# The head of a fused spectral and feed-forward kernel: squares, transforms and products in another order, and the last down weights in six pieces

## The chip, the cores and the metric

The kernel runs on one core of a Trainium2 chip. The metric is the device time of one execution in microseconds (us). The engines are TensorE (PE in the profile, with PEld for its weight loads), VectorE (DVE), ScalarE (ACT), GpSimd (POOL) and SyncE (SP), which here issues nearly all transfers.

## The reference

```python
def _A_ref(x, w_r, w_i):
    X = rfft2(x.astype(float32), axes=(-2, -1))
    W = w_r + 1j * w_i
    return irfft2(X * W, s=(S, D), axes=(-2, -1)).astype(bfloat16)

def _B_ref(x, w_gate, w_up, w_down):
    return (_gelu(x @ w_gate) * (x @ w_up)) @ w_down

h = x + _A_ref(_layernorm(x), A_w_r, A_w_i)
return h + _B_ref(_layernorm(h), B_w_gate, B_w_up, B_w_down)
```

S is 2048 rows, D is 576 columns and the hidden width is 4608. Everything is bf16. The input `B_x` is not used. The first line is a filter in the frequency domain, done with matrix products; the second is a gated feed-forward layer.

## The kernel before, in words

The 2048 rows lie in `h_sb` as 16 tiles of 128 rows; tile h holds the rows h, h + 16 and so on. The spectral part transforms, multiplies by the weights and transforms back. Its last step is a transform over the columns, `inv_cols(x, g)`, for two halves x and eight groups g: ten matrix products into a PSUM buffer and one copy out, on ACT except for (1, 1), which is on DVE. `add_rows(g)` then combines both halves of group g into two PSUM buffers, one for tile 2g and one for 2g + 1, and these are added to `h_sb`.

All of these PSUM buffers, those of the turns and those of the feed-forward products have one tag, `two`, with four buffers. They are handed out in turn in the order of the program, so a matrix product that opens a buffer waits until the reader of the buffer four openings earlier is done.

The feed-forward part works on four blocks of 512 rows (`tcnk`). For each of them `gate` computes 36 column blocks f of the hidden width: 18 matrix products for gate and up, a Gelu on ACT into `g_sb` and a multiplication on DVE (L895) into `P_sb`. Then the down products of four tiles follow, with the weights `wd[f // 12]`, which lie in three parts of 12 blocks. Gate and up weights come in groups of three column blocks (`load_gu`, two transfers each) into three buffers; group n is loaded when the last block of group n - 3 is done.

The head is the seam of the two parts. So that PE need not wait until four tiles are ready, the first eight column blocks of the first 512 rows are done in two halves: first for tiles 0 and 1 (the loop over `NH`), and later, as the first eight blocks of the main loop, for tiles 2 and 3. Tiles 0 and 1 get their mean and variance from a sum that comes with the addition (`add_sum`) and a sum of squares (`sum_squares`, on ACT), put together by `head_rstd` (three small instructions on DVE and a power on POOL). They are normalised (`norm_row`), transposed by PE (`turn_mm`) and copied into the layout that `gate` reads by DVE (`turn_out`). Tiles 2 and 3 are normalised by `norm2` and transposed by a transfer (`flip`, issued by SP).

The order of each engine is that of the program text: the schedule is manual. Work of the main loop that is not a product is put in by the table `todo`, whose key is the number of the block behind which it is issued: the folding and adding of later tiles, their statistics, their normalised rows and their flips. The table `after` does the same for the eight first half blocks. SP has one queue and works in order of the program: an issue that waits holds up the issues behind it.

Of the kernel before, what the change touches and what calls it, by code (L numbers as in the profile page):

```python
# [9 lines left out]
ACT = mybir.ActivationFunctionType  # L10
ALU = mybir.AluOpType
FP32 = mybir.dt.float32
BF16 = mybir.dt.bfloat16
# [7 lines left out]
P = 128  # L21
S = 2048
H = 16
D = 576
# [17 lines left out]
def kernel_body(  # L42
# [11 lines left out]
    nc = tc.nc  # L54
    V = nc.vector
    A = nc.scalar
# [4 lines left out]
    keep = ctx.enter_context(tc.tile_pool(name="keep", bufs=1))  # L61
    wgpool = ctx.enter_context(tc.tile_pool(name="wgu", bufs=3))
    roll = ctx.enter_context(tc.tile_pool(name="roll", bufs=2))
    psum = ctx.enter_context(tc.tile_pool(name="psum", bufs=1, space=bass.MemoryType.PSUM))

    def two(name):
        return psum.tile([P, 2, 512], FP32, name=name, tag="two", bufs=4)

    h_sb = keep.tile([P, H, D], BF16, name="h_sb")
# [6 lines left out]
    def const(name, val):  # L76
        t = keep.tile([P, 1], FP32, name=name)
        V.memset(t[:], val)
        return t

    zerob = const("zerob", 0.0)
# [30 lines left out]
    sums = keep.tile([P, H, 2], FP32, name="sums")  # L112
# [43 lines left out]
    wd_view = B_w_down.rearrange("(ft p) d -> p ft d", p=P)  # L156
    NWA = 12
# [479 lines left out]
    def inv_cols(x, g):  # L637

        ps = two("cs_ps")
        for w in range(NW):  # L640
            for e in range(2):
                rows = slice(64 * e, 64 * e + JW)
                T.matmul(  # L643
                    ps[:, e, 0:JP],
                    lhsT=EO[x][rows, w, 2 * g : 2 * g + 2].rearrange("p h e k l -> p (h e k l)"),
                    rhs=DQ[rows, w] if w or e else DT[rows, 0, :, 0, :],
                    start=(w == 0),
                    stop=(w == NW - 1),
                )
        pv = ps[:, :, 0:JP].rearrange("p t (q a) -> p t q a", q=2)  # L650
        if g >= 2:
            if x == 0 or g == 2:
                cw[x, g] = eop.tile([P, 2, JP], FP32, name=f"cw{x}{g}")[:]
            else:
                cw[x, g] = cwb[:, g - 3]
            A.activation(
                cw[x, g].rearrange("p t (a q) -> p t q a", q=2), pv, ACT.Copy, scale=Y_SCALE
            )
            return
        ts = eop.tile([P, 2, JP], BF16, name=f"cs{x}{g}")  # L660
        dst = ts[:].rearrange("p t (a q) -> p t q a", q=2)
        if x == 1 and g == 1:
            V.tensor_scalar(dst, pv, Y_SCALE, None, op0=ALU.mult)
        else:
            A.activation(dst, pv, ACT.Copy, scale=Y_SCALE)
        cs[x, g] = ts
# [58 lines left out]
    wd = [wd_a] + [fp.tile([P, NWA, D], BF16, name=f"wd_{i}") for i in range(2)]  # L725

    def load_wd(i):
        nc.sync.dma_start(wd[i][:], wd_view[:, i * NWA : (i + 1) * NWA, :])
# [5 lines left out]

    load_wd(1)


    ln2 = {}
    both = {}
# [13 lines left out]
    def add_rows(g):  # L753


        ys = [two("y_ps") for _ in range(2)]
        sl = (slice(0, DH), slice(DH, 0, -1))
        for x in range(2):
            for b in range(2):
                for t in range(2 if g < 2 else 1):  # L760
                    for i in range(2):
                        rows = slice(64 * i, 64 * i + 64)
                        T.matmul(  # L763
                            ys[i][:, b, 0:DH],
                            lhsT=G16[rows, b * t, x, :],
                            rhs=cs[x, g][rows, t, sl[b]] if g < 2 else both[x, g][rows, b, :],
                            start=(x == 0 and t == 0),
                            stop=(x == 1 and (g >= 2 or t == 1)),
                        )
        return ys  # L770
# [33 lines left out]
    def add_sum(h, ys, squares=True):  # L804


        hv = h_sb[:, h, :].rearrange("p (b n) -> p b n", b=2)
        V.scalar_tensor_tensor(  # L808
            hv, ys[h % 2][:, :, 0:DH], 1.0, hv, op0=ALU.mult, op1=ALU.add, accum_out=sums[:, h, 0:1]
        )  # L810
        if squares:
            sum_squares(h)

    def sum_squares(h):
        junk = roll.tile([P, D], BF16, name="junk", tag="junk", bufs=2)
        A.activation(junk[:], h_sb[:, h, :], ACT.Square, scale=float(D) ** 0.5, accum_out=sums[:, h, 1:2])  # L816

    def head_rstd(h):


        V.scalar_tensor_tensor(
            mv2[:, h, 1:2], sums[:, h, 0:1], sums[:, h, 0:1], sums[:, h, 1:2], op0=ALU.mult, op1=ALU.subtract
        )
        V.tensor_scalar(rstd2[:, h : h + 1], mv2[:, h, 1:2], -1.0 / (D * D), 1e-5, op0=ALU.mult, op1=ALU.add)
        V.tensor_scalar(mv2[:, h, 0:1], sums[:, h, 0:1], 1.0 / D, None, op0=ALU.mult)
        G.tensor_tensor(rstd2[:, h : h + 1], rstd2[:, h : h + 1], mhalf[:, h : h + 1], ALU.pow)  # L826

    def turn_mm(h):
        pt = psum.tile([P, 2048], BF16, name="pt", tag="two", bufs=4)
        for r in range(NR):  # L830
            for p0 in (0, 64):
                T.transpose(pt[p0 : p0 + 64, r * P : (r + 1) * P], ln2[h][:, r * 64 : (r + 1) * 64], ident[:])  # L832
        return pt
# [5 lines left out]
    def norm_row(h):  # L839
        hrow = ln2[h] = roll.tile([P, D], BF16, name="hflat", tag="hrow", bufs=4)  # L840
        normalise(V, hrow[:], mv2, rstd2, h)

    inv_cols(1, 0)
    inv_cols(1, 1)
    A.activation(keep.tile([P, 1], FP32, name="first_gelu")[:], zerob[:], ACT.Gelu_apprx_tanh)
    y0 = add_rows(0)
    add_sum(0, y0)
    add_sum(1, y0)
    head_rstd(0)
    head_rstd(1)  # L850
    for x, g in ((0, 6), (0, 7), (1, 2), (1, 3)):
        inv_cols(x, g)
    norm_row(0)
    norm_row(1)
    pt0 = turn_mm(0)
    inv_cols(1, 4)
    pt1 = turn_mm(1)
    turn_out(0, pt0)
    turn_out(1, pt1)
# [5 lines left out]
    todo = {}  # L865
    for h in range(4, H):
# [6 lines left out]
        todo.setdefault(b, []).append((norm2, h))  # L873
        todo.setdefault(b + 1, []).append((flip, h))

    blk = 0
    groups = pre
    NG = NFT // FQ

    def gate(tcnk, f, w, i, lo, hi):  # L880
        n = hi - lo
        gu = two("gu")
        for r in range(NR):
            for c in range(2):
                rows = slice(64 * c, 64 * c + 64)
                T.matmul(  # L886
                    gu[:, c, 0:n],
                    lhsT=w[rows, r, i * P : (i + 1) * P],
                    rhs=hl[tcnk % 2][rows, r, lo:hi],
                    start=(r == 0),  # L890
                    stop=(r == NR - 1),
                )
        g_sb = roll.tile([P, D], FP32, name="g_sb", tag="g_sb", bufs=3)[:, 0:n]
        A.activation(g_sb, gu[:, 0, 0:n], ACT.Gelu_apprx_tanh)  # L894
        V.tensor_tensor(p_sb(f)[:, lo:hi], g_sb, gu[:, 1, 0:n], ALU.mult)  # L895

    NH = 8
    after = {
        0: [(sum_squares, 3), (norm2, 2), (flip, 2), (head_rstd, 3)],
        1: [(norm2, 3), (flip, 3), (load_wd, 2)],  # L900
    }
    for f in range(NH):
        gate(0, f, groups[f // FQ], f % FQ, 0, 2 * P)
        for fn, h in after.get(f, ()):
            fn(h)
        if 2 <= f <= 4:
            inv_cols(1, f + 3)
    for tcnk in range(4):
        for gi in range(NG):
            for i in range(FQ):  # L910
                f = gi * FQ + i
# [51 lines left out]
@with_exitstack  # L963
def kernel(
    ctx: ExitStack,
    tc: tile.TileContext,
    A_x: bass.AP,
    A_w_r: bass.AP,
    A_w_i: bass.AP,
    B_x: bass.AP,  # L970
    B_w_gate: bass.AP,
    B_w_up: bass.AP,
    B_w_down: bass.AP,
    out: bass.AP,
):
    kernel_body(tc, A_x, A_w_r, A_w_i, B_x, B_w_gate, B_w_up, B_w_down, out)
# [30 lines left out]
```

## Time and profile before

| what | value |
|---|---|
| median of three runs | 500.94 us (500.82 to 501.02) |
| the profiled execution | 501.55 us |
| its span | 499.8 us |
| PE busy | 489.0 us, 98% of the span |
| DVE, ACT, POOL busy | 222.7, 162.9, 29.2 us |
| granted clock of TensorE | 1.0 in all of the span |
| PE busy, 62.0 to 79.15 us | 15.76 of 17.15 us |
| PE busy, 79.15 to 90.4 us | 10.50 of 11.25 us |
| PE busy, 90.4 to 145 us | 54.60 of 54.60 us |
| mean share of the transfer engines, 104 to 133.25 us | 1.08, 193 GB/s |

Times in the profile count from the start of the span. The span is what the engines were seen to do; the execution's own time has some microseconds around it. The views used are the page, the waits (who stood still until whom, in all, how often and the longest), the chain of waits (the work that ended last, followed back), the timeline (start, duration, engine, line, operation, count and in brackets the idle time before it with what ended it) and windows (the busy time of each engine, the granted clock, the share of the transfer engines in use and GB/s, in a stretch of time). The ends of matrix products are modelled, and neighbours overlap by about 0.2 us.

### The profile page before, as it was taken

How to read it: one execution, taken by the hardware profiler on the slowest of the kernel's cores; microseconds unless marked ns; L12 is line 12 of the kernel's file. 1: busy time of each engine (PE TensorE's matmuls, PEld its weight loads, DVE VectorE, ACT ScalarE, POOL GpSimd, SP SyncE). 2: the span in 40 equal slices, each digit the busy share in tenths (PEclk: the TensorE clock that was granted, in tenths of full speed). 3: DMA queues.
4: the chain of work that ended last, by engine and by line, in shares of the span. 5: the costliest groups of instructions: out<-in, count | busy, mean ns of one | idle time of the engine just before them, and what ended most of it. 6: DMA issues, size and time to landing. Idle time of an engine off the chain costs nothing.

```text
span 499.8 us, 12608 instructions
## 1 busy us (share of the span) xinstructions
PE 489.0 (98%) x5644; PEld 321.5 (64%) x5644; DVE 222.7 (45%) x440; ACT 162.9 (33%) x289; POOL 29.2 (6%) x78
## 2 busy tenths in 40 slices
PE   7999989999999999999999999999999999999997
PEld 3567779444469964444499944444799644445995
DVE  8989776788641235433311154333211333333111
ACT  8989973222320112323300133232110223233000
POOL 8500010111110000000000000000000000000000
PEclk9999999999999999999999999999999999999999
DMA  8729749999971019998740069987700287770000
GB/s 285 217 60 201 213 129 230 182 168 199 172 151 24 2 49 172 200 181 153 160 87 3 3 147 193 196 159 155 146 3 1 71 157 155 156 153 2 14 13 25
DMA packets 89469, 62.33 MB, mean 125 GB/s; under 512 B 23110, under 2 KB 88006, under 8 KB 89414
## 3 DMA queue, kind: packets, MB, share of 16 engines
q1 hardware_dynamic: 89126, 60.34, 59.6%
q0 software_dynamic: 288, 1.18, 0.7%
q8 instruction: 44, 0.72, 0.6%
q14 instruction: 11, 0.09, 0.1%
HBM read 52.65 MB, written 2.36 MB: 110 GB/s over the span
## 4 chain that ended last, share of the span: by engine, by line
PE 89%; DMA 2%; DVE 1%; ACT 0%; POOL 0%; issue 0%; SPq 0%; ACTq 0%
PE gu L886 54%; PE acc L928 26%; PE cs_ps L643 2%; PE acc L947 2%; PE eo_ps L592 2%; DMA wgu<-in_B_w_up_dram 2%; PE pq_ps L478 1%; PE y_ps L763 1%; PE gh_ps L496 0%; PE gh_ps L495 0%; DVE hrow L788 0%; PE pt L832 0%; PE eo_ps L616 0%; POOL rstd L826 0%; ACT junk L816 0%; DVE h_sb L808 0%
## 5 line engine op out<-in xcount | busy, mean ns | idle before, releaser
L886 PE MATMUL gu<-Bt,wgu 64*128 64x512 bf16 (+1 forms) x2736 | 284.1, 365 | 1.4 <-DMA wgu<-in_B_w_up_dram 0.7
L886 PEld LDWEIGHTS <-wgu 64*128 64x128 bf16 x2736 | 136.4, 94 | 145.2 <-DMA wgu<-in_B_w_up_dram 1.2
L895 DVE TENSOR_TENSOR P_sb<-g_sb,gu 128x512 bf16<-128x512 f32 (+1 forms) x152 | 99.6, 657 | 145.9 <-ACT g_sb L894 145.9
L894 ACT ACTIVATE g_sb<-gu 128x512 f32<-128x512 f32 (+1 forms) x152 | 87.3, 575 | 195.3 <-PE gu L886 195.1
L928 PEld LDWEIGHTS <-P_sb 64*128 64x128 bf16 x2160 | 132.7, 94 | 0.6
L928 PE MATMUL acc<-wd,P_sb 64*128 64x288 bf16 x1440 | 93.8, 283 | 0.0
L937 DVE TENSOR_TENSOR part<-part,acc 128x576 f32<-128x576 f32 x15 | 11.3, 754 | 111.3 <-ACT part L936 111.3
L928 PE MATMUL acc<-wd_a,P_sb 64*128 64x288 bf16 x720 | 49.7, 283 | 0.0
L936 ACT COPY part<-acc 128x576 f32<-128x576 f32 x15 | 9.6, 639 | 122.4 <-PE acc L928 122.4
L285 PE MATMUL f2t<-h_sb,ident 128*128 128x512 bf16 x27 | 9.1, 501 | 3.6 <-DMA h_sb<-in_A_x_dram 3.6
L478 PE MATMUL pq_ps<-DT,Bt 128*128 128x290 bf16 x64 | 12.2, 286 | 0.2 <-DVE Bt L327 0.2
L788 DVE TENSOR_SCALAR hrow<-h_sb,mv,rstd 128x1152 bf16<-128x1152 bf16 x14 | 12.1, 867 | 0.6 <-POOL rstd L826 0.6
L939 DVE TENSOR_TENSOR h_sb<-h_sb,part 128x576 bf16<-128x576 bf16 x15 | 11.4, 758 | 0.5
L643 PE MATMUL cs_ps<-DQ,EO 58*128 58x290 bf16 x144 | 11.3, 283 | 0.0
L133 POOL TENSOR_TENSOR rstd<-rstd,mhalf 128x1 f32<-128x1 f32 (+1 forms) x16 | 11.2, 701 | 1.3
L478 PEld LDWEIGHTS <-Bt 128*128 128x128 bf16 x96 | 9.3, 97 | 2.6
L132 POOL TENSOR_SCALAR rstd<-mv 128x1 f32<-128x1 f32 (+1 forms) x16 | 3.9, 246 | 102.6 <-DVE mv L118 102.4
L297 PE MATMUL f2t<-F,xn 128*128 128x256 bf16 x64 | 9.2, 274 | 0.6 <-DVE xn L136 0.6
L489 ACT CAST pq<-pq_ps 128x580 bf16<-128x580 f32 x15 | 9.6, 668 | 0.0
L123 ACT ACTIVATE junk<-h_sb 128x576 bf16<-128x576 bf16 x14 | 9.4, 676 | 0.4 <-DMA h_sb<-in_A_x_dram 0.4
L643 PEld LDWEIGHTS <-EO 58*128 58x128 bf16 x160 | 8.0, 94 | 2.0 <-issue 0.4
L117 DVE BATCH_NORM_STATS2 st<-h_sb 128x6 f32<-128x288 bf16 x21 | 9.3, 441 | 0.0
(133 smaller groups left out, 266.0 us busy)
## 6 DMA issues: line engine op xcount, KB each, us to landing
wgu<-in_B_w_gate_dram SPq DMA_DIRECT2D x48, 432.0 KB
wgu<-in_B_w_up_dram SPq DMA_DIRECT2D x48, 432.0 KB
wd<-in_B_w_down_dram SPq DMA_DIRECT2D x2, 1728.0 KB
wd_a<-in_B_w_down_dram SPq DMA_DIRECT2D x1, 1728.0 KB
out_dram<-h_sb SPq DMA_DIRECT2D x3, 576.0 KB
h_sb<-in_A_x_dram SPq DMA_DIRECT2D x4, 288.0 KB
h_sb<-in_A_x_dram SPq DMA_DIRECT2D x2, 576.0 KB
WR<-in_A_w_r_dram SPq DMA_DIRECT2D x1, 650.2 KB
```

The source lines that it names most:

```text
L133: G.tensor_tensor(dst[:, sl], dst[:, sl], mhalf[:, sl], ALU.pow)
L478: T.matmul(ps[:, par, 0:JP], lhsT=Bt[:, t, col], rhs=DT[:, t // 2, par] if t < 4 else DF[:, par], start=(t == par), stop=(t == 4),)
L592: T.matmul(pv[:, n], lhsT=z[:, a, w].rearrange("p b j -> p (b j)"), rhs=TI[:, ts[k], 1 - a : 3 - a, :], start=(a == 0), stop=(a == 1),)
L643: T.matmul(ps[:, e, 0:JP], lhsT=EO[x][rows, w, 2 * g : 2 * g + 2].rearrange("p h e k l -> p (h e k l)"), rhs=DQ[rows, w] if w or e else DT ...
L788: V.tensor_scalar(hrow[:], h_sb[:, h, :].rearrange("p (r k) -> p r k", k=64).unsqueeze(2).to_broadcast([P, NR, 2, 64]), mv2[:, h, 0:1], rs ...
L886: T.matmul(gu[:, c, 0:n], lhsT=w[rows, r, i * P : (i + 1) * P], rhs=hl[tcnk % 2][rows, r, lo:hi], start=(r == 0), stop=(r == NR - 1),)
L894: A.activation(g_sb, gu[:, 0, 0:n], ACT.Gelu_apprx_tanh)
L895: V.tensor_tensor(p_sb(f)[:, lo:hi], g_sb, gu[:, 1, 0:n], ALU.mult)
L928: T.matmul(accs[i][:, c, 0:DH], lhsT=p_sb(f)[rows, st * P : (st + 1) * P], rhs=wd[f // NWA][rows, f % NWA, c * DH : (c + 1) * DH], start=( ...
L937: V.tensor_tensor(part, part, accs[1][:, :, 0:DH], ALU.add)
L939: V.tensor_tensor(hv, hv, part, ALU.add)
L947: T.matmul(acc[:, 0, 0:DH], lhsT=p_sb(f)[:, st * P : (st + 1) * P], rhs=wd[f // NWA][:, f % NWA, cc], start=(f == 0), stop=(f == NFT - 1),)
```

## The change

Seven things are different, all between the last column transforms and the middle of the first 36 blocks.

- The squares of tile 1 are computed by DVE, with one instruction that multiplies the tile by itself and sums up, instead of by ACT.
- Six column transforms, (0, 6), (0, 7) and (1, 2) to (1, 5), stand between the addition of tiles 0 and 1 and their turns. Before, four stood there, (1, 4) stood between the two turns and (1, 5) behind the third gate block.
- The two turns follow each other.
- The first Gelu, which brings ACT's table load, comes behind the copies of these six transforms.
- In the half blocks, `head_rstd(3)` comes behind block 1 instead of block 0, and tile 3's row and its flip behind block 2 instead of block 1.
- (1, 6) and (1, 7) come behind half blocks 2 and 3, where before (1, 5) to (1, 7) came behind 2 to 4.
- The last third of the down weights, which was one transfer behind tile 3's flip, is six transfers of two blocks each, behind blocks 10, 13, 16, 19, 22 and 25 of the main loop.

```diff
+    def load_wd2(s):
+        nc.sync.dma_start(wd[2][:, s], wd_view[:, 2 * NWA : 3 * NWA][:, s])
...
     inv_cols(1, 0)
     inv_cols(1, 1)
-    A.activation(keep.tile([P, 1], FP32, name="first_gelu")[:], zerob[:], ACT.Gelu_apprx_tanh)
     y0 = add_rows(0)
     add_sum(0, y0)
-    add_sum(1, y0)
+    add_sum(1, y0, squares=False)
+    for x, g in ((0, 6), (0, 7), (1, 2), (1, 3), (1, 4), (1, 5)):
+        inv_cols(x, g)
+    A.activation(keep.tile([P, 1], FP32, name="first_gelu")[:], zerob[:], ACT.Gelu_apprx_tanh)
+    junk = roll.tile([P, D], BF16, name="junk", tag="junk", bufs=2)
+    V.scalar_tensor_tensor(
+        junk[:], h_sb[:, 1, :], float(D), h_sb[:, 1, :], op0=ALU.mult, op1=ALU.mult, accum_out=sums[:, 1, 1:2]
+    )
     head_rstd(0)
     head_rstd(1)
-    for x, g in ((0, 6), (0, 7), (1, 2), (1, 3)):
-        inv_cols(x, g)
     norm_row(0)
     norm_row(1)
     pt0 = turn_mm(0)
-    inv_cols(1, 4)
     pt1 = turn_mm(1)
     turn_out(0, pt0)
     turn_out(1, pt1)
...
+    for i in range(0, NWA, 2):
+        todo.setdefault(10 + 3 * i // 2, []).append((load_wd2, slice(i, i + 2)))
...
     after = {
-        0: [(sum_squares, 3), (norm2, 2), (flip, 2), (head_rstd, 3)],
-        1: [(norm2, 3), (flip, 3), (load_wd, 2)],
+        0: [(sum_squares, 3), (norm2, 2), (flip, 2)],
+        1: [(head_rstd, 3)],
+        2: [(norm2, 3), (flip, 3)],
     }
     for f in range(NH):
         gate(0, f, groups[f // FQ], f % FQ, 0, 2 * P)
         for fn, h in after.get(f, ()):
             fn(h)
-        if 2 <= f <= 4:
-            inv_cols(1, f + 3)
+        if 2 <= f <= 3:
+            inv_cols(1, f + 4)
```

## The prediction

> **What bounds the kernel now.** I read the page first: PE is busy for 98% of the span and the granted clock is 1.0 everywhere, so only time in which PE stands still, or order that makes it stand still, can be won. Then the waits of 58 to 95 us, the stretch that the edit touches.
>
> ```profile
> PE gu L886 <- DMA wgu<-in_B_w_up_dram: 0.7, 1, 0.7
> PE pt L832 <- DVE hflat L136: 0.7, 1, 0.7
> PE gu L886 <- DVE P_sb L895: 0.7, 1, 0.7
> ```
>
> Three waits of PE. The timeline of PE places them:
>
> ```profile
> 62.00 0.28 PE L643 MATMUL cs_ps<-DT,EO 58*128 58x290 bf16 x1
> ...
> 65.39 0.69 PE L832 MATMUL pt<-ident,hflat 128*64 128x128 bf16 x18 [0.73 <-DVE hflat L136]
> 66.02 0.29 PE L643 MATMUL cs_ps<-DT,EO 58*128 58x290 bf16 x1
> ...
> 74.41 1.16 PE L886 MATMUL gu<-Bt,wgu 64*128 64x256 bf16 x18 [0.66 <-DVE P_sb L895]
> ...
> 76.02 8.04 PE L886 MATMUL gu<-Bt,wgu 64*128 64x256 bf16 x144
> ...
> 90.38 4.05 PE L886 MATMUL gu<-Bt,wgu 64*128 64x512 bf16 x35 [0.75 <-DMA wgu<-in_B_w_up_dram]
> ```
>
> The first is for tile 0's normalised row, the second for a PSUM buffer that a multiplication (L895) frees, the third for gate/up group 3. What DVE does ahead of the second:
>
> ```profile
> 72.09 0.21 DVE L821 SCALAR_TENSOR_TENSOR mv<-sums 128x1 f32<-128x1 f32 x1
> ...
> 72.47 0.41 DVE L895 TENSOR_TENSOR P_sb<-g_sb,gu 128x256 bf16<-128x256 f32 x1
> 73.16 0.87 DVE L788 TENSOR_SCALAR hrow<-h_sb,mv,rstd 128x1152 bf16<-128x1152 bf16 x1 [0.28 <-POOL rstd L826]
> 73.95 0.74 DVE L895 TENSOR_TENSOR P_sb<-g_sb,gu 128x256 bf16<-128x256 f32 x2
> ```
>
> Tile 3's row (73.16) stands ahead of the third product (73.95). SP and the transfers around it (of the windows only DMA share and GB/s, the last two columns, matter):
>
> ```profile
> 72.21 3.10 SPq L800 DMA_TRANSPOSE Bt<-hrow  x2
> 75.36 0.64 SPq L728 DMA_DIRECT2D wd<-in_B_w_down_dram  x1
> 82.12 0.62 SPq L144 DMA_DIRECT2D wgu<-in_B_w_gate_dram  x1
> ```
>
> ```profile
> 73.25:74.75 1.50, 0.84 (x15) 0.61 (x13) 1.44 (x3) 0.98 (x2) 0.00 (x0) 1.00 1.34 172
> ...
> 75.25:76.50 1.25, 1.25 (x26) 1.20 (x24) 0.42 (x1) 0.65 (x2) 0.00 (x0) 1.00 1.16 227
> ...
> 78.50:82.25 3.75, 3.75 (x73) 3.75 (x71) 1.95 (x5) 1.36 (x5) 0.00 (x0) 1.00 1.07 367
> ...
> 88.15:97.25 9.10, 8.35 (x81) 4.04 (x79) 5.83 (x14) 2.14 (x4) 1.35 (x3) 1.00 1.12 196
> ```
>
> The two transposes flow one after the other; the down weights end at about 82.3 (a trickle lasts to 83.25); then groups 3, 4 and 5 fill the engines to 97.25.
>
> **The change part by part.** *Head, 62.0 to 68.4.* After the four transforms PE stands from their modelled end (64.66) to 65.39. Two more transforms, (1,4) and (1,5), now come ahead of the turns. One takes 0.62 (starts 62.00, 62.62, 63.24, 63.87), so PE is through at 65.72. (1,4) only moves within the head; (1,5) leaves the gates.
>
> Does the row wait longer? Square 0 stays on ACT (62.99, accumulator at 63.77). Square 1 goes to DVE behind the second sum (ends 63.63). The trace has no such instruction on two bf16 tensors; bounds are 0.43 (the row's TENSOR_SCALAR at L136, one bf16 source) and 0.87 (hrow, twice the elements). I take 0.76, the same operation at the same 576 elements, L808, though its source is PSUM. So DVE is free at 64.43, not 63.80, and the statistics (three instructions and POOL's power) follow: statistics 0 until 64.87, POOL's power 0.56 until 65.46, row 0 by 65.94 (0.43), turn 0 at 65.99. PE waits 0.27 there. The second power ends at 66.06 and row 1 at 66.5, before PE wants it at 66.62. Turn 1 ends at 67.25 (before: 67.37).
>
> The next work, row group 1, needs two PSUM buffers. The fourfold rotation gives it those of (1,4) and (1,5), so it now waits for ACT's copy of (1,5). ACT starts copying at 63.67 instead of 64.35, as one square is gone, and copies at 0.56 to 0.62 pitch (L656: three in 1.81): the sixth ends between 67.2 and 67.5. So row group 1 starts at 67.25 to 67.5; I take 67.37, as before, and gate 0 at 68.39, as before. Bounds: 0.12 won, 0.13 lost. The turn's copies on DVE (0.76 each) end at 68.2 and hide. The Gelu table load (1.28, with 0.20 for the first Gelu) moves from 61.44, where ACT would have idled, to behind the six copies, ending by 69.0; the next square needs ACT at 69.42, so its cover is 0.4.
>
> *Gates 0 to 7.* Before, with three transforms between them, blocks of the main loop begin at 76.02 + 3 x 0.98 = 78.97. Now 68.39 + 8 x 0.983 + 2 x 0.618 = 77.49, if nothing waits. The 1.48 won is 0.62 for the transform and 0.86 for the wait at 74.41 with its refill. Does that wait go? New order on DVE: product 0 (70.62), row 2 (71.31 to 72.18, needing square 2 and POOL as before), product 1 (to 72.50), statistics 3 (to 72.90), product 2 (to 73.23), row 3 behind POOL's power (0.56) from 73.50 to 74.37, product 3 (to 74.7). Buffers are then wanted from product 0 at 71.96 (free 71.0), 1 at 72.96 (72.5), 2 at 73.57 (73.2) and 3 at 75.5 (74.7). It goes. ACT only changes the place of copies.
>
> What is late next is tile 3's transpose. Blocks 0 to 7 of the main loop read tiles 2 and 3. SP issued it at 74.06 and now issues it at 74.40, while its reader comes 1.48 earlier, 3.09 after the issue instead of 4.9. In the windows the data end 2.5 after an issue (72.21 to 74.75; 74.06 to 76.5). Landing after the last byte: the first input chunk flowed until about 3.0 and ACT started on it at 3.62, 0.6; against that, WI's copy flowed at speed until 21.75 and POOL's work on it started at 23.51, 1.76. With 0.6 the transpose lands at 77.5; with 1.76, at 78.66. The wait is 0 to 1.2. I take 0.2, nearer the first row, since the queue is empty here too.
>
> *Down weights.* One issue (0.64) goes; six come behind groups 5 and 6 and then behind transposes and loads in blocks 10 to 25. SP pays 0.4 to 0.64 each and spends 155 us waiting for PE, so that hides. First reader: block 24 of the first accumulation, after 151 us; the last piece is issued near 126.
>
> Group 3 is the other end. Its load is issued when block 2 ends and is wanted seven blocks later, both unchanged against each other: 82.11 to 89.6, landed 90.33. Is the 0.75 caused by the down weights? Group 3 reached full flow 2.4 after its issue (84.5), group 6 into an empty queue 2.1 (96.90 to 99.0). So removing them gains 0 to 0.3; I take 0.1. Nearly all of this wait stays.
>
> The pieces join loads that run nearly full: from 104 to 133 the share is about 1.1. A piece is 295 KB, 0.8 us at 367 GB/s, and the holes in which nothing much flows (97.25 to 98.25, 103.25 to 104, 110.25 to 111.25, 122.5 to 123.25) sum to 3.5 of the 4.8 us that six need. A load has 12.1 us from issue to reader there (six blocks of 1.95 and a row group of 0.46); group 3, with the queue full, took 8.2 (82.12 to 90.33 in the chain). So 3.9 covers the rest: nothing, bounds 0 and 5.6 (worked out under the rivals).
>
> Sum: 1.48 - 0.2 + 0.1 = 1.4 us. The profiled execution took 501.55, 1.75 more than its span, and lies 0.6 above the median; it gives 500.15, and the same against the median gives 499.6.
>
> **The rivals.** *A transpose that lands late* takes the place of the wait removed: with WI's 1.76 the wait is 1.2, the gain 0.4 and the time 500.5; halfway, 500.1. For it: the margin falls by 1.8 us. Against: the first chunk's 0.6. The Trainium skill (DMA: Bandwidth & Descriptors, Anatomy of one DMA) says that a transfer's semaphore fires only after the write receipt, most of a fixed 2 us, which it gives for the GpSimd path. By that rule, as an estimate, landing would come 1.5 us or more after the last byte, the wait would be about 0.9 and the time about 500.3. The trace has both: 0.6 disagrees, 1.76 agrees.
>
> *Slower:* the pieces make group loads late. At 196 GB/s, the rate at which group loads flow together, a piece costs 1.5, six cost 9.0; minus 3.5 of holes and 3.9 of slack, PE waits 1.6 near block 24, and the time is 501.1. Where a transpose stands ahead it can be more: a load issued at 192.41 behind one flowed from 194.5, 2.1 later, where group 3 took 1.1. Another 1.0 for the four pieces behind transposes makes the wait 5.6 and the time 505.1; midway, 503. Waiting begins at 1.2 us a piece and outweighs the 1.4 won from about 1.5. Against: the single load ran at 367.
>
> *Group 3 no longer waits,* if the trickle to 83.25 held one engine back: 0.75 and its refill, together 0.9 more, 498.8. Against: others ramp as slowly.
>
> *The buffer wait only moves* (PE stands for (1,5)'s copy, or for a product): the transform's 0.62 alone remains, less 0.2: 500.5.
>
> **How the numbers follow.** Forecast 0.52 (499.2 to 499.9), late transpose 0.21, buffer wait 0.06, slower 0.14, group 3 gone 0.07. 0.2% is 1.0 us, about what a measurement of this kernel can tell. Faster by more: 0.52 + 0.07 + 0.03 of the late transpose, 0.62. Same: its other 0.18, 0.06 of the buffer wait, and 0.04 of the slower case, which between 501.1 and 501.9 can't be told from no change: 0.28. Slower: the remaining 0.10. The range leaves out the slower case and little of the fastest: 498.8 to 500.7.
>
> **What would show it.** Right: turn 0 waits some 0.3 instead of 0.73; no wait for a product near 74; main-loop blocks begin near 77.5 on a transpose issued at 74.4; group 3 still waits 0.5 to 0.8. Wrong: a wait of PE behind the transposes of over 0.6, a load other than group 3 that PE waits for, or group 3's wait gone.

## The result and the profile after

The changed kernel takes 499.93 us, the median of 22 runs (499.47 to 501.26). The kernel before, beside it, takes 501.0 (500.63 to 501.88). The ratio is 0.998, with a 95% interval of 0.9973 to 0.9987: 1.0 us faster, between 0.65 and 1.35. The forecast was 1.4 us, with a range of 498.8 to 500.7.

The profiled execution took 499.93 us, its span is 498.1, 1.7 less than the span of the profile before. Lines of the kernel have moved: the gate products are L894 (before L886), the products on DVE L903 (L895), the transposes L803 (L800), the pieces L738. These are the waits of PE for which the prediction had shown its three, and one wait of its weight loads:

```profile
PE gu L894 <- DMA wgu<-in_B_w_up_dram: 0.5, 1, 0.5
...
PEld L835 <- DVE hflat L136: 0.3, 1, 0.3
...
PE gu L894 <- DMA Bt<-hrow: 0.2, 1, 0.2
```

The wait for a product's buffer is gone, the one for row 0 is down to 0.3, group 3's is smaller, and there is a new one, for tile 3's transpose. The timeline of PE:

```profile
62.00 0.28 PE L643 MATMUL cs_ps<-DT,EO 58*128 58x290 bf16 x1
...
65.94 1.22 PE L835 MATMUL pt<-ident,hflat 128*64 128x128 bf16 x36
67.09 1.33 PE L766 MATMUL y_ps<-cs,G 64*128 64x288 bf16 x16
68.17 3.21 PE L894 MATMUL gu<-Bt,wgu 64*128 64x256 bf16 x54
...
73.35 4.20 PE L894 MATMUL gu<-Bt,wgu 64*128 64x256 bf16 x72
77.77 5.09 PE L894 MATMUL gu<-Bt,wgu 64*128 64x256 bf16 x90 [0.23 <-DMA Bt<-hrow]
...
88.90 4.06 PE L894 MATMUL gu<-Bt,wgu 64*128 64x512 bf16 x35 [0.46 <-DMA wgu<-in_B_w_up_dram]
```

PE does the six transforms without a gap (they start 0.62 apart, from 62.00 to 65.11), the turns at 65.94, gate 0 at 68.17 (before 68.39), the main loop at 77.77 (before 78.97) and group 3's first block at 88.90 (before 90.38). On DVE the new square took 0.76, as estimated, and the third product now stands ahead of tile 3's row:

```profile
63.67 0.76 DVE L855 SCALAR_TENSOR_TENSOR junk<-h_sb 128x576 bf16<-128x576 bf16 x1
...
72.60 0.41 DVE L903 TENSOR_TENSOR P_sb<-g_sb,gu 128x256 bf16<-128x256 f32 x1
73.29 0.87 DVE L791 TENSOR_SCALAR hrow<-h_sb,mv,rstd 128x1152 bf16<-128x1152 bf16 x1 [0.28 <-POOL rstd L829]
```

On SP, the two transposes, group 3's load, and then one place where the six pieces show:

```profile
72.00 4.28 SPq L803 DMA_TRANSPOSE Bt<-hrow  x2
80.93 0.63 SPq L144 DMA_DIRECT2D wgu<-in_B_w_gate_dram  x1
...
122.62 5.40 SPq L803 DMA_TRANSPOSE Bt<-hrow  x1
128.07 0.58 SPq L738 DMA_DIRECT2D wd<-in_B_w_down_dram  x1
128.75 0.63 SPq L144 DMA_DIRECT2D wgu<-in_B_w_gate_dram  x1
```

The transpose behind block 24 now holds SP for 5.40 us. In the profile before it took 2.20, and group 11 was issued at 127.02:

```profile
123.32 2.20 SPq L800 DMA_TRANSPOSE Bt<-hrow  x1
127.02 0.65 SPq L144 DMA_DIRECT2D wgu<-in_B_w_gate_dram  x1
```

With all else about 1.4 us earlier, group 11 was due near 125.6 and is issued at 128.75. Its weights land as PE comes for them, 8.81 us after that: PE's weight loads wait 0.4 us, and the chain gives the stretch of six blocks there 11.77 us instead of 11.69.

```profile
137.56 3.35 PEld L894 LDWEIGHTS <-wgu 64*128 64x128 bf16 x34 [0.40 <-DMA wgu<-in_B_w_up_dram]
```

The gain stands in the chain of waits at the first accumulation. The work from there on is the same in both kernels and stays 1.40 apart up to the last products; the other 0.3 of the two spans lies behind those. Before, then after:

```profile
145.36 35.25 PE acc L928 x574
```

```profile
143.96 35.25 PE acc L937 x574
```

### The profile page after: what moved, and what is told of

The parts are those of the page before. It is cut to its first block, busy times and chain, and to the rows that moved or that the text cites. A ratio compares the mean times of both kernels' runs of the same rounds, so it can differ in the third digit from the quotient of the medians.

```text
span 498.1 us, 12611 instructions
## 1 busy us (share of the span) xinstructions
PE 489.0 (98%) x5642; PEld 320.1 (64%) x5644; DVE 223.2 (45%) x442; ACT 162.0 (33%) x287; POOL 29.3 (6%) x78
## 4 chain that ended last, share of the span: by engine, by line
PE 90%; DMA 2%; ACT 0%; SPq 0%; issue 0%; DVE 0%
PE gu L894 54%; PE acc L937 27%; PE cs_ps L643 2%; PE acc L956 2%; PE eo_ps L592 2%; DMA wgu<-in_B_w_up_dram 1%; PE pq_ps L478 1%; PE y_ps L766 1%; DMA Bt<-hrow 1%; PE gh_ps L496 0%; PE gh_ps L495 0%; PE eo_ps L616 0%; PE pt L835 0%; ACT hs L514 0%; SPq L144 0%; ACT pq L489 0%
## 5 line engine op out<-in xcount | busy, mean ns | idle before, releaser
L894 PE MATMUL gu<-Bt,wgu 64*128 64x512 bf16 (+1 forms) x2736 | 284.5, 365 | 0.7 <-DMA wgu<-in_B_w_up_dram 0.5
L894 PEld LDWEIGHTS <-wgu 64*128 64x128 bf16 x2736 | 135.0, 94 | 146.1 <-DMA wgu<-in_B_w_up_dram 1.4
L903 DVE TENSOR_TENSOR P_sb<-g_sb,gu 128x512 bf16<-128x512 f32 (+1 forms) x152 | 99.6, 657 | 144.7 <-ACT g_sb L902 144.7
L791 DVE TENSOR_SCALAR hrow<-h_sb,mv,rstd 128x1152 bf16<-128x1152 bf16 x14 | 12.1, 867 | 0.6 <-POOL rstd L829 0.6
```

The lines of the kernel that those rows point to most:

```text
L791: V.tensor_scalar(hrow[:], h_sb[:, h, :].rearrange("p (r k) -> p r k", k=64).unsqueeze(2).to_broadcast([P, NR, 2, 64]), mv2[:, h, 0:1], rs ...
L894: T.matmul(gu[:, c, 0:n], lhsT=w[rows, r, i * P : (i + 1) * P], rhs=hl[tcnk % 2][rows, r, lo:hi], start=(r == 0), stop=(r == NR - 1),)
```

## The experiments

Row group 0 (the first row products) starts at 60.8 to 61.4 us of the span in these profiles, though no version changes the work ahead of it, so this table counts from its start. "Main loop" is the start of block 0 of the main loop, taken as 4.91 us (five half blocks) ahead of the row products of group 2; "accumulation" is the first line of it in the chain. Both are of one profiled execution each, in us. The ratio is of the timed runs, to the kernel before as it ran beside that version: its median was 501.0 beside the changed kernel, 501.04 and 501.05 beside the parts, 501.35 beside the last two rows.

| version | main loop | accumulation | median | ratio, 95% interval |
|---|---|---|---|---|
| before | 17.96 | 84.35 | 501.0 | |
| before, again | 17.97 | 83.94 | 501.13 (1 run) | |
| head alone | 17.42 | 83.24 | 500.71 | 0.9995 (0.9985 to 1.0004) |
| products alone | 17.95 | 84.04 | 501.11 | 1.0002 (0.9993 to 1.0011) |
| pieces alone | 17.97 | 84.07 | 500.89 | 0.9998 (0.9989 to 1.0007) |
| products and pieces | 17.92 | 84.03 | 500.82 | 0.9993 (0.9984 to 1.0002) |
| head and products, one load | 16.97 | 84.19 | 501.04 | 1.0005 (0.9994 to 1.0016) |
| changed | 16.76 | 82.95 | 499.93 | 0.998 (0.9973 to 0.9987) |
| changed, again | 16.91 | 83.12 | 500.06 | 0.9974 (0.9963 to 0.9985) |
| changed, squares on ACT | 17.84 | 84.22 | 500.86 | 0.9988 (0.9979 to 0.9997) |

**The parts by themselves.** Four kernels ran beside each other. The first has the head of the change, with the old table and the old load (against the changed kernel):

```diff
-    for i in range(0, NWA, 2):
-        todo.setdefault(10 + 3 * i // 2, []).append((load_wd2, slice(i, i + 2)))
...
-        0: [(sum_squares, 3), (norm2, 2), (flip, 2)],
-        1: [(head_rstd, 3)],
-        2: [(norm2, 3), (flip, 3)],
+        0: [(sum_squares, 3), (norm2, 2), (flip, 2), (head_rstd, 3)],
+        1: [(norm2, 3), (flip, 3), (load_wd, 2)],
```

> The head alone (squares of tile 1 on DVE, six transforms ahead of the turns, first Gelu later); the products and the down weights as in the kernel before. Theory (two independent gains, the order of the head and the order of the products): turn 0 waits 0.2 as in the changed kernel, gate 0 starts near 68.2, the wait for a product's buffer stays at 0.6 to 0.8, blocks of the main loop begin near 78.3 instead of 78.97; 0.5 to 0.7 us faster than the kernel before. Rival (only the pieces matter, through group 3): within 0.2 us of before. Rival (the head's order alone removes the buffer wait too): 1.2 us faster.

Measured: 0.25 us faster, an interval of 0.75 faster to 0.2 slower. In its profile the product's buffer is waited for as before (0.6), and the main loop comes 0.54 earlier, near the 0.67 of the theory. At the first accumulation it comes even 0.7 to 1.1 earlier than in the two profiles of the kernel before. But row group 0 starts 0.39 later in this execution, at 61.40, and the timed runs show a quarter of a microsecond, below the theory's range. So the worth of the head alone is known only within these figures.

The second has the old head and the new table of products, with the one load behind tile 3's flip (against the kernel before):

```diff
-        0: [(sum_squares, 3), (norm2, 2), (flip, 2), (head_rstd, 3)],
-        1: [(norm2, 3), (flip, 3), (load_wd, 2)],
+        0: [(sum_squares, 3), (norm2, 2), (flip, 2)],
+        1: [(head_rstd, 3)],
+        2: [(norm2, 3), (flip, 3), (load_wd, 2)],
```

> The products ahead of tile 3's row alone; head and down weights (one load behind tile 3's flip) as before. Theory: the wait of 0.66 near 74.4 with its refill goes, blocks of the main loop begin near 78.1, no wait for tile 3's transpose (its reader comes 3.7 after the issue, it lands 3.5 after); but the whole load of the down weights then lies closer ahead of group 3, so that wait grows from 0.75 by up to 0.4: 0.4 to 0.8 us faster. Rival (only the pieces matter): within 0.2 us of before.

Measured: no difference. This is a miss of the theory, and the timeline of PE shows why:

```profile
73.36 1.17 PE L886 MATMUL gu<-Bt,wgu 64*128 64x256 bf16 x18
...
74.97 3.13 PE L886 MATMUL gu<-Bt,wgu 64*128 64x256 bf16 x54
78.75 5.09 PE L886 MATMUL gu<-Bt,wgu 64*128 64x256 bf16 x90 [0.65 <-DMA Bt<-hrow]
```

The wait of 0.66 for a buffer went and one of 0.65 for tile 3's transpose stands in its place. The transpose was issued at 74.18 and its reader started at 78.75, 4.57 later; in the changed kernel these are 74.19, 77.77 and 3.58.

The third has the six pieces alone (the load taken out of the table, the six put into `todo`):

> The down weights in six pieces alone; head and products as before. Theory: group 3's wait falls from 0.75 by 0.3, no new wait of PE in blocks 10 to 36, tile 3's transpose lands as before: 0.2 to 0.4 us faster. Rival (the down weights cause group 3's wait): the wait is gone, 0.9 us faster. Rival (the pieces make loads late): slower, with a wait for a load near blocks 18 to 30.

Measured: no difference, and the profile shows that two things cancel. At group 3 no product waits any more (its weight loads wait 0.4), and from the start of row group 2 to the products behind row group 3 it takes 10.13 us, where the two profiles of the kernel before took 10.92 and 10.50. The wait is gone as in the first rival, but the gain isn't there: PE now waits for group 11, issued at 129.65 behind a transpose that holds SP for 5.39, as the second rival had it, only later in the loop:

```profile
130.32 8.11 DMA wgu<-in_B_w_up_dram
138.47 3.97 PE gu L891 x35
```

From 118.10 to 142.90 this kernel needs 24.80 us for two stretches of six blocks with their row groups, the kernel before 24.29: 0.51 is lost there. The same place costs 0.34 with products and pieces and 0.25 with the squares on ACT, against 0.09 and nothing in the two profiles of the changed kernel.

The fourth is the change without the pieces:

```diff
-    for i in range(0, NWA, 2):
-        todo.setdefault(10 + 3 * i // 2, []).append((load_wd2, slice(i, i + 2)))
...
-        2: [(norm2, 3), (flip, 3)],
+        2: [(norm2, 3), (flip, 3), (load_wd, 2)],
```

> The whole change but for the pieces: the last third of the down weights is one load behind tile 3's flip. Theory: the load is issued near 76.3, ends near 83.5 and is now in the way of group 3, which is issued near 80.9: its wait is 1.2 to 1.8 instead of 0.46, and the kernel is only 0.2 to 0.7 us faster than before. Rival (the pieces are worth what they were worth before the head moved, 0.3): group 3 waits 0.75, 1.0 to 1.2 us faster than before.

Measured: no faster than before at all, below the theory's range, its median 1.1 us above the changed kernel's. The wait for group 3 is the one of the theory, and one for the transpose came beside it. PE's waits and the issues on SP:

```profile
PE gu L892 <- DMA wgu<-in_B_w_up_dram: 1.6, 1, 1.6
PE gu L892 <- DMA Bt<-hrow: 0.5, 1, 0.5
```

```profile
71.98 4.38 SPq L803 DMA_TRANSPOSE Bt<-hrow  x2
76.41 0.58 SPq L728 DMA_DIRECT2D wd<-in_B_w_down_dram  x1
81.14 0.63 SPq L144 DMA_DIRECT2D wgu<-in_B_w_gate_dram  x1
```

The load is issued 1.05 later than before (75.36) and group 3 is issued 0.98 earlier (82.12). What just passed ahead of group 3 in the kernel before now runs into it: over 350 GB/s, the rate of the single load, flow until 83.25, 2.1 us after group 3's issue, and the group lands 9.1 after its issue, where it took 7.7 to 8.3 in the other versions whose products wait for it. So the pieces are worth nothing on the whole by themselves and 1.1 us behind the other two parts.

Head and pieces without the new order of products wasn't run. So it isn't shown by a timed run that the change needs the products. In the profiles the main loop of head and products comes 0.45 earlier than that of the head alone, and those of the two profiles of the changed kernel 0.66 and 0.51.

**Why the transpose lands late.** The products with the pieces and the old head, so with nothing behind the transposes:

> The products' order and the six pieces, with the head as before. Theory (the down weights right behind tile 3's transpose are what made it land 4.6 us after its issue in the run of the products alone, against 3.6 in the changed kernel): the transpose lands 3.5 to 3.7 after its issue, the reader comes 3.9 after it, so its wait is gone or under 0.1, blocks of the main loop begin 0.8 us earlier than before, and the kernel is 0.4 to 0.9 us faster. Rival (the transpose takes 4.6 for another reason, such as row 2's flow ahead of it): wait of 0.6 as with the products alone, within 0.2 us of before.

The theory fell; the kernel is 0.35 us faster than before, between 0.8 faster and 0.1 slower. The transpose was issued at 74.18 and its reader started at 78.72 after a wait of 0.62: 4.54 again, without any down weights near. The windows show where the time goes. First this version, then the changed kernel (the last two columns are DMA share and GB/s):

```profile
75.25:76.50 1.25, 1.25 (x28) 1.25 (x25) 0.15 (x1) 0.96 (x2) 0.00 (x0) 1.00 1.05 193
76.50:77.75 1.25, 1.25 (x28) 1.25 (x25) 0.60 (x2) 0.44 (x2) 0.00 (x0) 1.00 1.35 24
77.75:78.00 0.25, 0.25 (x7) 0.07 (x2) 0.24 (x1) 0.00 (x0) 0.00 (x0) 1.00 0.80 160
```

```profile
75.25:76.00 0.75, 0.75 (x20) 0.67 (x16) 0.22 (x1) 0.38 (x1) 0.00 (x0) 1.00 1.06 159
76.00:76.50 0.50, 0.50 (x14) 0.45 (x10) 0.42 (x1) 0.00 (x1) 0.00 (x0) 1.00 1.14 35
76.50:77.25 0.75, 0.75 (x18) 0.67 (x14) 0.23 (x1) 0.38 (x1) 0.00 (x0) 1.00 0.97 211
```

In both, the transfer of tile 3 stands still in its middle while the engines count as busy: 1.25 us with 24 GB/s in the one, about half a microsecond with 35 GB/s in the other. An instruction fetch of 0.02 MB lies in the transpose's flow in the first (76.0 to 76.5) and ahead of it in the second (74.5 to 75.0). But the changed kernel run again and the folded version (below) have the fetch ahead too and a stall of 0.5 to 1.0, and the version with the row later has it there and none. So what makes it stand still stays open.

**Whose transpose.** Tile 3's row and flip moved behind half block 3, one execution:

```diff
-        2: [(norm2, 3), (flip, 3)],
+        3: [(norm2, 3), (flip, 3)],
```

> The changed kernel with tile 3's row and flip one half block later (behind block 3 instead of 2). Theory (the wait of 0.23 at the first main-loop block is for tile 3's transpose): its issue moves by the products in between, 0.6 to 1.0, and PE's wait grows by the same, to 0.8 to 1.2; the landing stays 3.5 to 3.7 behind the issue. Rival (the wait is for tile 2's transpose or for a buffer): 0.2 to 0.3 as now.

The issue moved by 0.42 only (74.61; one product that was ready went ahead), the wait was 0.46, and the transpose landed 3.34 after its issue. This doesn't decide between theory and rival: the unchanged kernel waits 0.23 in one profile and 0.38 in another (below). That PE waits for tile 3's transpose rests on the windows: its bytes are the last ahead of group 3's load, they end near 77.2, and PE starts 0.5 to 0.8 behind them. The time of this execution was 499.99 us.

**The square.** The changed kernel with the square of tile 1 back on ACT:

```diff
-    add_sum(1, y0, squares=False)
+    add_sum(1, y0)
...
-    junk = roll.tile([P, D], BF16, name="junk", tag="junk", bufs=2)
-    V.scalar_tensor_tensor(
-        junk[:], h_sb[:, 1, :], float(D), h_sb[:, 1, :], op0=ALU.mult, op1=ALU.mult, accum_out=sums[:, 1, 1:2]
-    )
```

> The changed kernel with the squares of tile 1 back on ACT; everything else as changed. Theory (the square on DVE pays by letting ACT copy the transforms sooner, since the buffers of row group 1 are those of the last two transforms): statistics come earlier and turn 0 waits 0 to 0.1 instead of 0.2, but the six copies start 0.68 later, the sixth ends near 67.9 and row group 1 waits for it; gate 0 starts 0.5 to 0.7 later than in the changed kernel, and so does the end: 0.4 to 0.7 us slower than the changed kernel. Rival (the copies had slack, so the place of the square doesn't matter): same as the changed kernel within 0.2.

Measured: 500.86 against 500.06 of the changed kernel beside it, 0.8 slower, and gate 0 at 68.81 instead of 68.15. The cause is the one of the theory, ACT's copies starting 0.68 later, but it strikes earlier than expected, where transform (1, 4) wants the buffer of (0, 6):

```profile
65.06 0.28 PE L643 MATMUL cs_ps<-DT,EO 58*128 58x290 bf16 x1 [0.41 <-ACT cw L656]
```

So DVE's square pays by making ACT free, not by being quicker: it delays the statistics.

**The two kernels again.** Both unchanged, profiled a second time:

> The kernel before, unchanged, profiled a second time. Theory (the profile of before that the prediction was made from showed a longer wait for group 3 than is usual, which is why the profiles differ by 1.7 us of span and the medians by 1.1): the wait for group 3 is 0.1 to 0.5 instead of 0.75, the waits for row 0 and for the product's buffer stay at 0.73 and 0.66, the time is near the median, 500.7 to 501.2. Rival (the wait is always 0.75): it is 0.7 to 0.8 again.

> The changed kernel, unchanged, timed and profiled again beside the others. Theory (its wait for tile 3's transpose follows where an instruction fetch falls, and group 3's landing and group 11's late issue vary from execution to execution): the order of waits is the same (transpose 0.2 to 0.6, group 3 0.2 to 0.6, group 11 issued 2 to 4 us late), with sizes that differ by some tenths; 0.9 to 1.2 us faster than before. Rival (the first comparison was of one chip): under 0.5 or over 1.5 faster.

The kernel before now takes 501.13 us and waits 0.33 for group 3, with the same issue at 82.12 and the same other waits, as the theory had it:

```profile
89.96 3.41 PE L886 MATMUL gu<-Bt,wgu 64*128 64x512 bf16 x30 [0.33 <-DMA wgu<-in_B_w_up_dram]
```

The changed one waits 0.38 for the transpose and 0.56 for group 3, and its transpose behind block 24 holds SP for 5.41 again. It is 1.3 us faster than before in these runs (interval 0.75 to 1.85). Group 3 landed 8.26 and 7.84 us after its issue in the two profiles of the kernel before and 7.97 and 8.08 in those of the changed one, each pair with the same program. The two pairs of profiles differ by 1.40 and 0.82 at the first accumulation, on the mean 1.1, near the 1.1 and 1.3 by which the medians differ.

**Towards a better version.** Three variations of the changed kernel. The first puts row group 3's products into the place where PE waits for group 3:

```diff
-            todo.setdefault((1, 6, 10, 13, 16, 19)[h // 2 - 2], []).append((fold, h // 2))
-            todo.setdefault(b + 4, []).append((add_both, h // 2))
+            todo.setdefault((1, 3, 10, 13, 16, 19)[h // 2 - 2], []).append((fold, h // 2))
+            todo.setdefault(8 if h == 6 else b + 4, []).append((add_both, h // 2))
```

> The changed kernel, with the folding of row group 3 behind block 3 instead of 6 and its row products (0.46 us of PE) behind block 8 instead of 10, into the place where PE waits for group 3's load. Theory (the group lands 7.7 to 8.0 after its issue whatever lies around): the wait falls from 0.46 to under 0.1 and the kernel is 0.3 to 0.5 us faster than the changed one, 1.3 to 1.6 faster than before. Rival (the wait is of PE's refill or the load follows PE's order): no gain, 1.0 to 1.1 faster than before.

Measured: 500.17 (ratio to before 0.9977, 0.9968 to 0.9986), no gain over the changed kernel. PE's wait for group 3 is gone and another came, for a cause that the expectation hadn't priced: the folding, 1.5 us of DVE in the main loop, holds up a product, and PE waits for its buffer.

```profile
84.99 4.08 PE L894 MATMUL gu<-Bt,wgu 64*128 64x256 bf16 x54 [0.45 <-DVE P_sb L903]
```

The second keeps the pieces away from the transposes of tiles 4 to 7:

```diff
-    for i in range(0, NWA, 2):
-        todo.setdefault(10 + 3 * i // 2, []).append((load_wd2, slice(i, i + 2)))
+    for i, b in enumerate((10, 10, 13, 13, 28, 31)):
+        todo.setdefault(b, []).append((load_wd2, slice(2 * i, 2 * i + 2)))
```

> The changed kernel with the six pieces behind blocks 10, 10, 13, 13, 28 and 31, so that none lies among the transposes of tiles 4 to 7 (blocks 15 to 24). Theory (the pieces there lengthen the issue of the transposes on SP, up to 5.4 us, so that group 11 is issued 3 us late and lands when PE wants it; in some executions later): the transposes' issues are 1.3 to 2.3 as before, group 11 is issued within 0.2 of the end of its block, no wait near 137, the largest time of the runs falls below 500.6 and the median is 0.1 to 0.4 us below the changed kernel's. Rival (the late group never costs): same median and the same spread as the changed kernel's.

Measured: 499.73, of six runs between 499.50 and 500.14 (ratio 0.997, 0.9958 to 0.9982). Group 11 is issued at 126.52 instead of 128.75, still 0.7 late, and the wait near 137 is gone. The transposes still hold SP for 2.5 to 4.8 us, which the theory had wrong: pieces that are issued well ahead of them lengthen them too. The third adds to the second the foldings of groups 2 and 3 in half blocks 4 and 6, where DVE idles, and the products behind block 8:

```diff
-            todo.setdefault((1, 6, 10, 13, 16, 19)[h // 2 - 2], []).append((fold, h // 2))
-            todo.setdefault(b + 4, []).append((add_both, h // 2))
+            if h > 6:
+                todo.setdefault((10, 13, 16, 19)[h // 2 - 4], []).append((fold, h // 2))
+            todo.setdefault(8 if h == 6 else b + 4, []).append((add_both, h // 2))
...
+        4: [(fold, 2)],
+        6: [(fold, 3)],
```

> The changed kernel with the pieces as in the spread version (blocks 10, 10, 13, 13, 28, 31), the folding of row groups 2 and 3 behind half blocks 4 and 6, where DVE has idle time, and row group 3's products behind block 8, where PE waits for group 3's load. Theory (the filled version gave nothing because the folding, put among the main blocks, held up a product and made PE wait 0.45 for its buffer): no wait for a product near 85, wait for group 3 under 0.1, 0.3 to 0.6 us faster than the changed kernel. Rival (what is saved at group 3 is lost at the next load): a wait near block 12, same as the changed kernel.

Measured: 499.81 of six runs (499.01 to 500.17; ratio 0.9968, 0.9956 to 0.998), beside 500.06 of the changed kernel. PE's waits for group 3 and for a product are gone as expected, and the first accumulation comes 82.65 after row group 0, the earliest of all. What remains is the wait for tile 3's transpose, 0.66 in this execution. The intervals of both variations overlap with the changed kernel's, so neither is shown to beat it.

## Why the prediction was right, and what it missed

The direction and the order of size held: 1.0 us came of the 1.4 forecast in the first runs and 1.3 in the second. The first pair of profiles differs by 1.40 at the first accumulation, but that this is the forecast's own sum is luck. By its steps it is 0.22 + 1.48 - 0.50 + 0.28 - 0.08, and of these terms only the 1.48 was forecast so:

- *Head, 0 with bounds of 0.12 won and 0.13 lost.* It was 0.22 won (68.39 to 68.17), past the bound. The two turns in a row took 1.15 us, where the sum had two times 0.63, and ACT's six copies ended at 67.2, its faster end. The square was 0.76, as taken.
- *Gates 0 to 7, 1.48.* Right: without the next wait the main loop would have begun at 68.17 + 8 x 0.983 + 2 x 0.618 = 77.27, which is 1.70 early, of which 0.22 is the head's. The buffer's wait went.
- *Tile 3's transpose, 0.2 with bounds 0 and 1.2.* This is the term that was too small. The listed wait is 0.23 and 0.38 in the two profiles, but the main loop began 0.50 and 0.66 behind the time so worked out (77.27 and 77.25; the ends of products are modelled and overlap, so the listed idle time is less than the loss). The landing was 3.3 to 4.6 us after the issue over the profiles here, within the bounds' 3.1 to 4.3 or just past them. What was mis-sized is the flow: the sum let the data end 2.5 after the issue, and they ended 2.8 to 3.1 after it in the two profiles of the changed kernel and 3.6 to 3.8 with products and pieces, mostly by the stall in the transfer's middle. So the rival of a late transpose was half true, by another road than its own. Its 1.76 for WI's copy was misread: the windows show 54 to 9 GB/s trickling on until 23.0, half a microsecond before POOL started, so most of it was flow too. The rule of the Trainium skill that stood beside it (DMA: Bandwidth & Descriptors, Anatomy of one DMA: the write receipt makes most of the fixed 2 us, given there for the GpSimd path) is not what the windows of these transposes show. In the changed kernel the data ended between 77.0 and 77.25 and PE started at 77.77, so 0.5 to 0.8 lay behind the last byte, where the sum had 0.6; the delay was in the flow.
- *Group 3, 0.1 won, nearly all of the wait stays.* It stayed: 0.46 and 0.56. Against the 0.75 of the profile it is 0.28 won at that place (1.20 became 1.48), between the second profiles it is 0.23 lost (0.33 became 0.56). The prediction took one execution's 0.75 as the kernel's.
- *Pieces, nothing, bounds 0 and 5.6.* Nearly nothing against the kernel before: 0.08 at block 33. But the mechanism of the slower rival was there, by another road than its own: not too many bytes alone, but SP held for 5.4 us by a transpose issue. Group 11 was issued 3.2 us late and took 8.8 to land, which used up its 12.1 us. The prediction's sign "a load other than group 3 that PE waits for" thus came in a small way here, and with 0.51 in the version with the pieces alone.

The sum was of independent terms, and the experiments show that they aren't. Head alone gives 0.25 (at most 0.75), products alone and pieces alone nothing that the runs can tell, and the change without the pieces nothing; all together give 1.0. The pieces were costed against the kernel before, where the load passes just ahead of group 3. There they win some tenths at group 3 and lose them at group 11; with the other parts, which bring load and group together, they are worth 1.1. The products, too, gain only with the new head: with the old one the transpose lands 4.54 and 4.57 after its issue and takes the place of the wait removed. Why it lands later there is open.

## What to carry to other kernels

Cost each part of a change also in the kernel that the other parts leave: a load that just passes ahead of another is free only as long as nothing moves. When a wait is removed, measure the margin of the next one by its landing, and count stalls inside a transfer as part of it. Take the size of a transfer wait from several executions, since 0.4 us of it came and went here with no change of the program.

## What the runs showed that was not expected

A DMA transpose of 295 KB, behind only tile 2's transpose on the queue, landed between 3.3 and 4.6 us after its issue (the start of the PE product that waits for it), in kernels that all issue it between 73.9 and 74.8; in two of them the down weights follow it. Most of the difference is a stretch of 0 to 1.25 us in which its engines count as busy and little flows (24 and 35 GB/s in the windows shown).

SP's issue of a transpose took 1.3 us where nothing else was on the queue (tile 2's) and up to 5.65 behind loads and pieces (the folded version), and everything behind it on SP waits that long.
